# Seven products instead of eight for seven of the twelve column blocks of a SwiGLU

## The chip, the cores and the metric

The kernel runs on one core of one Trainium2 chip. The metric is the device time of one execution in microseconds, a median over runs. The core's engines work from queues of their own: PE multiplies matrices, DVE, ACT and POOL do elementwise work, SP issues most transfers.

## What is computed

Three layers follow one another on 1152 tokens of 512 values: a retention layer, a mixture of eight experts, and a SwiGLU. The change lies in the last one:

```
rms = np.sqrt(np.mean(x * x, axis=-1, keepdims=True) + 1e-06)
xn = x / rms * rms_g
g = xn @ w_gate                      # 1152x512 by 512x1536
silu = g * (1.0 / (1.0 + np.exp(-g)))
val = xn @ w_val                     # 1152x512 by 512x1536
return (silu * val @ w_out)          # 1152x1536 by 1536x512
```

The three weight matrices of this layer are float64 in memory; the result is float32.

## The kernel before

**Stages.** Attention and routing take the first 60 us or so, the experts run to about 214 us, the SwiGLU from there to the end. Only the last stage changes its work.

**Numbers in two parts.** Each float32 operand is split into a rounded high part (`xh`, `uh`, `sh`; ACT writes it) and the rest (`xl`, `ul`, `sl`; DVE subtracts it), and a product is three matmuls: high by high, high by low, low by high.

**Items.** The 1536 columns are twelve blocks `f` of 128, the tokens three groups `g` of 384. An item (g, f) is `gate_val` (L1120 to L1122: 24 matmuls of 384 columns, into one PSUM bank for gate and one for value, each held twice), `gate_act` (L1130 silu on ACT, L1132 the product on DVE, L1134 and L1136 the two parts) and `out_mm` two items later (L1154 to L1156: nine matmuls of 512 columns into three PSUM tiles). There are 36 items in three phases: f 0 and 1, f 2 to 5, f 6 to 11. At a phase's end `out_ev` moves the three tiles of a group into `parts` (ACT in phase 0, DVE afterwards), and in the last phase POOL scatters them to the output.

**Conversion.** For each f three units (gate, value, output weights) are fetched as 64-bit words (`st`, four buffers) and turned into float32 by `conv_u`: ACT takes the upper word's magnitude (L233), DVE masks the sign (L238) and joins the words (L249, L257), then ACT and DVE make `uh` and `ul` (L265, L268). The generator is cut into three steps a unit; `between` puts them among the four pieces of `gate_act`, so many an item as `G_OPS` says by phase. All of this order is written by hand: each engine executes what the program lists for it in that order.

## Time and profile before

| | us |
|---|---|
| median of 3 runs (450.11 to 454.2) | 450.31 |
| the profiled execution's own time | 449.34 |
| its span, first to last instruction | 447.6 |
| PE busy | 432.2 |

The trace shows one execution. A matmul's record overlaps the next one's; what a matmul costs in a row of them is the distance from its start to the next one's. The same holds for DVE, by a little. Where a row names a line, it is a line of the kernel before.

### The profile page before, as it was taken

The page shows a single profiled execution, that of the slowest core. Times are in us where ns is not written, and L with a number is a line of the kernel's source. Part 1 is how long each engine was busy: PE and PEld are TensorE (multiplying, and loading weights), DVE is VectorE, ACT ScalarE, POOL GpSimd, SP SyncE. Part 2 cuts the span into 40 slices and gives each one's busy share as a digit, 9 for nine tenths or more (in the row PEclk, how much of TensorE's full clock was granted, in tenths as well). Part 3 has the DMA queues.
Part 4 walks back from the last instruction along what each step waited for, and adds up shares of the span by engine and source line. Part 5 has one row for each costly group of instructions (what it writes and reads, how often), then busy time and mean ns, then how long its engine had stood idle before and what let it go on. Part 6 is the DMA issues. An engine that isn't in the chain of part 4 may idle for free.

```text
span 447.6 us, 7844 instructions
## 1 busy us (share of the span) xinstructions
PE 432.2 (97%) x2976; PEld 410.5 (92%) x2976; DVE 285.5 (64%) x677; ACT 211.0 (47%) x453; POOL 56.1 (13%) x45
## 2 busy tenths in 40 slices
PE   6999989899999999999999999999999999999994
PEld 5888879899999999999999999999999999999993
DVE  3899857668888878786498888784763113113212
ACT  3443335778787877764466665350531111111110
POOL 8005210122441101012000000000000002001102
PEclk9999999899999999999999999999999999999999
DMA  8989829976999897673045564351300001000101
GB/s 284 306 280 379 314 82 346 327 230 143 367 184 348 245 308 256 244 256 116 1 140 175 156 187 143 112 173 45 94 1 0 0 2 70 1 1 21 51 1 70
DMA packets 40446, 72.28 MB, mean 162 GB/s; under 512 B 3894, under 2 KB 16566, under 8 KB 40404
## 3 DMA queue, kind: packets, MB, share of 16 engines
q1 hardware_dynamic: 38580, 67.00, 47.3%
q0 software_dynamic: 1824, 4.75, 2.9%
q8 instruction: 24, 0.39, 0.4%
q14 instruction: 18, 0.15, 0.1%
HBM read 65.21 MB, written 6.52 MB: 160 GB/s over the span
## 4 chain that ended last, share of the span: by engine, by line
PE 81%; DMA 2%; POOL 0%; DVE 0%; issue 0%; POOLq 0%; ACT 0%; DVEq 0%
PE gv L1120 11%; PE gv L1121 11%; PE gv L1122 11%; PE acc L914 11%; PE hp L623 9%; PE o L1154 5%; PE o L1156 5%; PE o L1155 5%; PE acc L915 4%; PE hp L863 3%; DMA xr<-tab 2%; PE hp L865 1%; PE tp L828 1%; PE sp L980 1%; POOL out_dram L1169 0%; PE sp L960 0%
## 5 line engine op out<-in xcount | busy, mean ns | idle before, releaser
L1120 PE MATMUL gv<-xh,uh 128*128 128x384 f32 x280 | 94.8, 339 | 0.0
L1122 PE MATMUL gv<-xh,ul 128*128 128x384 f32 x280 | 94.6, 338 | 0.0
L1121 PE MATMUL gv<-xl,uh 128*128 128x384 f32 x280 | 94.6, 338 | 0.0
L914 PE MATMUL acc<-h,w2h 128*128 128x384 f32 (+6 forms) x256 | 73.2, 360 | 0.0
L915 PE MATMUL acc<-h,w2l 128*128 128x192 f32 (+6 forms) x256 | 62.1, 243 | 0.0
L1132 DVE TENSOR_TENSOR sg<-sg,gv 128x384 f32<-128x384 f32 x35 | 19.3, 551 | 63.8 <-PE gv L1122 59.6
L1120 PEld LDWEIGHTS gv<-xh,uh 128*128 128x128 f32 x280 | 52.6, 188 | 1.4
L1121 PEld LDWEIGHTS gv<-xl,uh 128*128 128x128 f32 x280 | 52.6, 188 | 1.4
L1134 ACT ACTIVATE sh<-sg 128x384 fp32r<-128x384 f32 x36 | 18.9, 526 | 73.2 <-DVE sg L1132 73.1
L1122 PEld LDWEIGHTS gv<-xh,ul 128*128 128x128 f32 x280 | 52.6, 188 | 0.0
L623 PE MATMUL hp<-xt,w1t 128*128 128x192 f32 (+6 forms) x336 | 51.2, 306 | 0.6 <-DVE fl L644 0.6
L915 PEld LDWEIGHTS acc<-h,w2l 128*128 128x128 f32 x256 | 49.8, 195 | 0.0
L914 PEld LDWEIGHTS acc<-h,w2h 128*128 128x128 f32 x256 | 49.0, 191 | 0.0
L623 PEld LDWEIGHTS hp<-xt,w1t 128*128 128x128 f32 x336 | 47.5, 190 | 1.0 <-ACT h L889 0.8
L1154 PE MATMUL o<-uh,sh 128*128 128x512 f32 x108 | 42.8, 396 | 0.0
L1156 PE MATMUL o<-uh,sl 128*128 128x512 f32 x108 | 42.7, 395 | 0.0
L1155 PE MATMUL o<-ul,sh 128*128 128x512 f32 x108 | 42.5, 393 | 0.0
L1130 ACT ACTIVATE sg<-gv 128x384 f32<-128x384 f32 x35 | 17.0, 487 | 49.4 <-PE gv L1122 49.4
L787 DVE TENSOR_TENSOR w2l<-w2t,w2h 128x1024 fp32r<-128x1024 f32 x32 | 38.9, 1214 | 0.1
L778 ACT ACTIVATE w2h<-w2t 128x512 fp32r<-128x512 f32 x64 | 36.5, 620 | 3.4 <-DVEq L735 3.4
L1169 POOL DMA_INDIRECT out_dram<-part,ids_sb x9 | 8.9, 984 | 215.1 <-DVE part L1167 214.2
L265 ACT ACTIVATE uh<-mag 128x512 fp32r<-128x512 f32 x36 | 22.6, 627 | 14.7 <-DVE mag L257 10.0
(172 smaller groups left out, 727.5 us busy)
## 6 DMA issues: line engine op xcount, KB each, us to landing
w1t<-in_moe_w_dram SPq DMA_DIRECT2D x16, 1024.0 KB, 10.0
w2t<-in_moe_w_dram SPq DMA_DIRECT2D x32, 512.0 KB, 6.4
...
```

The source lines that it names most:

```text
L265: nc.scalar.activation(out=uh[:, s, :], in_=mag, func=ACTF.Copy)
L623: nc.tensor.matmul(hp[:, a, 0:w], w1_t[e, j // 2][:, kk, f * FT:(f + 1) * FT], xt[:, kk, :], start=(kk == 0), stop=(kk == KD - 1))
L778: nc.scalar.activation(out=w2_s[e, j][0][:, a, :], in_=t[:, a, :], func=ACTF.Copy)
L787: nc.vector.tensor_tensor(out=lo, in0=t, in1=hi.bitcast(F32), op=ALU.subtract)
L914: nc.tensor.matmul(ac[d // 2][:, d % 2, 0:2 * w], hi[:, a, d * P:(d + 1) * P], h[:, a].rearrange("p s t -> p (s t)"), start=first, stop=Fa ...
L915: nc.tensor.matmul(ac[d // 2][:, d % 2, 0:w], lo[:, a, d * P:(d + 1) * P], h[:, a, 0, :], start=False, stop=last, skip_group_check=True)
L1120: nc.tensor.matmul(ps[:, 0:GT], w_h, x_h, start=(kk == 0), stop=False)
L1121: nc.tensor.matmul(ps[:, 0:GT], w_h, x_l, start=False, stop=False)
L1122: nc.tensor.matmul(ps[:, 0:GT], w_l, x_h, start=False, stop=(kk == KD - 1))
L1154: nc.tensor.matmul(o, a, uh[:, 2, :], start=(f == fs[0]), stop=False)
L1155: nc.tensor.matmul(o, a, ul[:, 2, :], start=False, stop=False)
L1156: nc.tensor.matmul(o, b, uh[:, 2, :], start=False, stop=(f == fs[-1]))
```

## The change

**What stays plain.** Blocks f 0 to 4 are computed as before, in two phases (f 0 and 1; f 2 to 4), 15 items. `G_OPS` is now 6 conversion steps an item in the first and 7 in the second, and no bound holds conversion back: all twelve blocks are converted while these items run. For f 5 to 11 the float32 words are not split but written to memory (`raw_d`) by SP and read again when they are needed.

**Blocks of products.** For f 5 to 11 the gate and value columns are one 2 by 2 matrix of blocks (gate or value, first or second half of the 512 inputs), and the tokens are taken in two groups (`GROUPS`): twice 256, then twice 320. Of each group and f, called a slot (14 in all), the four result blocks come from seven block products with sums and differences of blocks on both sides. `prod` is one of them, six matmuls of 256 or 320 columns. POOL makes the sums: `x_split` for the tokens (six instructions a half, two halves for each of four tables; ACT and DVE split the results) and `w_sums` for the weights (four instructions a slot). `w_hi`, `w_lo`, `o_hi`, `o_lo` split the weights anew in each slot, and small additions on PSUM (rows `r<-q,m` and `m<-q,m`) join the products. The output matmuls of slot k - 1 stand in two halves within slot k; in the last slot they run from the last tile down, and one of them is kept for the end.

**Small things.** The constants that only attention reads lie in a pool that is closed after it. In the first two slots an extra matmul of 320 columns is issued ahead of the products.

**The order on PE.** Of the plain form, a piece of one item; the names are the tiles written and read.

```order
L1156 MATMUL o<-uh,sl 128x512
L1120 MATMUL gv_5409<-xh,uh 128x384
L1121 MATMUL gv_5409<-xl,uh 128x384
L1122 MATMUL gv_5409<-xh,ul 128x384
L1120 MATMUL gv_5409<-xh,uh 128x384
```

A slot's middle in the change: a second product into q, output tiles of the slot before, a third product into q.

```order
L1283 MATMUL q<-xh_5145,tl 128x256
L1305 MATMUL o<-oh,sh 128x512
L1306 MATMUL o<-ol,sh 128x512
L1307 MATMUL o<-oh,sl 128x512
L1305 MATMUL o<-oh,sh 128x512
L1306 MATMUL o<-ol,sh 128x512
L1307 MATMUL o<-oh,sl 128x512
L1281 MATMUL q<-xh_4927,th 128x256
```

The runs of 384 columns have become runs of 256 (later 320), with the output matmuls between them.

**The order on ACT, sixth item.** Before, conversion, the three copies of a group, the next silu:

```order
L233 ACTIVATE mag<-st 128x512
L265 ACTIVATE uh<-mag 128x512
L1165 ACTIVATE part_4810<-o 128x512
L1165 ACTIVATE part_4811<-o 128x512
L1165 ACTIVATE part_4812<-o 128x512
L1130 ACTIVATE sg<-gv_5025 128x384
```

In the change (L238 and L271 are the lines L233 and L265 of before):

```order
L238 ACTIVATE mag<-st 128x512
L1204 ACTIVATE xh_5145<-xd 128x4x128
L271 ACTIVATE uh<-mag 128x512
L1179 ACTIVATE part_4844<-o 128x512
L1179 ACTIVATE part_4845<-o 128x512
L1179 ACTIVATE part_4846<-o 128x512
L1144 ACTIVATE sg<-gv_5080 128x384
```

A copy of `xd`, which POOL writes, now stands ahead of the rounding, the copies and the silu.

**The order on DVE.** A piece of the last phase before:

```order
L1132 TENSOR_TENSOR sg<-sg,gv_6415 128x384
L1136 TENSOR_TENSOR sl<-sg,sh 128x384
L1132 TENSOR_TENSOR sg<-sg,gv_6457 128x384
L1136 TENSOR_TENSOR sl<-sg,sh 128x384
L1132 TENSOR_TENSOR sg<-sg,gv_6508 128x384
```

A slot of 256 columns in the change:

```order
L1331 TENSOR_TENSOR sg_6062<-sg_6062,q 128x256
L1342 TENSOR_TENSOR sl<-sg_6062,sh 128x256
L1342 TENSOR_TENSOR sl<-sg_6063,sh 128x256
L1451 TENSOR_TENSOR r<-q,m_6194 128x256
L1244 TENSOR_TENSOR tl<-raw,th 128x512
L1244 TENSOR_TENSOR tl<-raw,th 128x256
L1467 TENSOR_TENSOR m_6194<-q,m_6194 128x256
L1244 TENSOR_TENSOR tl<-ss,th 128x1024
L1481 TENSOR_TENSOR sg_6170<-sg_6170,m_6194 128x256
L1265 TENSOR_TENSOR ol<-raw,oh 128x512
```

Two instructions an item have become ten a slot.

```diff
-G_OPS = (6, 5, 5)
+G_OPS = (6, 7)
+GROUPS = ((0, 256), (512, 320))
...
-    A_U, B_U = 2, 6
+    A_U, SF = 2, 5
+    B_U = SF - A_U
...
-        return "A" if f < A_U or A_U + B_U <= f < 2 * A_U + B_U else "B"
+        return "A" if f < A_U else "B" if f < SF else "R"
...
-            nc.scalar.activation(out=uh[:, s, :], in_=mag, func=ACTF.Copy)
+            if plain:
+                nc.scalar.activation(out=w2u[f][0][:, s, :], in_=mag, func=ACTF.Copy)
 
         def lo():
+            if not plain:
+                return
+            uh, ul = w2u[f]
             nc.vector.tensor_tensor(out=ul[:, s, :], in0=mag, in1=uh[:, s, :].bitcast(F32), op=ALU.subtract)
 
+        if not plain:
+            nc.sync.dma_start(out=raw_d[f, s][:], in_=mag)
         tail[0] = (hi, lo)
+        tail_u[0] = (f, s)
...
-    phases = [list(range(0, A_U)), list(range(A_U, A_U + PH1)), list(range(A_U + PH1, NF2))]
-    order = [(ph, g, f) for ph in range(3) for g in range(NG) for f in phases[ph]]
+    phases = [list(range(0, A_U)), list(range(A_U, SF))]
+    order = [(ph, g, f) for ph in range(2) for g in range(NG) for f in phases[ph]]
...
+    def x_split(g, i, pool):
+        t0, n = GROUPS[g]
+        hn = n // 2
+        hi, lo = x_t[g, i] = [pool.tile([P, 4, n], F32R, tag=f"x{v}{g}{i}", name=f"x{v}{g}{i}") for v in "hl"]
+        for c in range(2):
+            xa = rxp.tile([P, 2, 2, NMX // 2], F32, tag="xa", name="xa")[:, :, :, 0:hn]
+            xd = rxp.tile([P, 4, NMX // 2], F32, tag="xd", name="xd")[:, :, 0:hn]
+            for k in range(2):
+                src = [t[:, 2 * k + i, t0:t0 + 2 * n].rearrange("p (h c) -> p h c", h=2)[:, :, c * hn:(c + 1) * hn].bitcast(F32) for t in (xh, xl)]
+                nc.gpsimd.tensor_tensor(out=xa[:, k], in0=src[0], in1=src[1], op=ALU.add)
+            nc.gpsimd.tensor_tensor(out=xd[:, 0], in0=xa[:, 0, 1], in1=xa[:, 0, 0], op=ALU.subtract)
+            nc.gpsimd.tensor_tensor(out=xd[:, 2], in0=xa[:, 1, 1], in1=xa[:, 0, 1], op=ALU.subtract)
+            nc.gpsimd.tensor_tensor(out=xd[:, 1], in0=xa[:, 1, 1], in1=xd[:, 0], op=ALU.subtract)
+            nc.gpsimd.tensor_tensor(out=xd[:, 3], in0=xa[:, 1, 0], in1=xd[:, 1], op=ALU.subtract)
+            yield
+            hi_v, lo_v = (t[:, :, c * hn:(c + 1) * hn] for t in (hi, lo))
+            nc.scalar.activation(out=hi_v, in_=xd, func=ACTF.Copy)
+            yield
+            nc.vector.tensor_tensor(out=lo_v, in0=xd, in1=hi_v.bitcast(F32), op=ALU.subtract)
...
+    def load_raw(k, js):
...
+                    conv_tail()
+                t = rawp.tile([P, 512], F32, tag="raw", name="raw")
+                nc.sync.dma_start(out=t, in_=raw_d[f, j][:])
...
+    def w_sums(k):
+        if k >= len(slots):
+            return
+        gt, vt = raw_t[k, 0], raw_t[k, 1]
+        a11, a12, a21, a22 = gt[:, 0:256], gt[:, 256:512], vt[:, 0:256], vt[:, 256:512]
+        ss = ssp.tile([P, 4, 256], F32, tag="ss", name="ss")
+        ss_t[k] = ss
+        nc.gpsimd.tensor_tensor(out=ss[:, 0], in0=a21, in1=a22, op=ALU.add)
+        nc.gpsimd.tensor_tensor(out=ss[:, 2], in0=a11, in1=a21, op=ALU.subtract)
+        nc.gpsimd.tensor_tensor(out=ss[:, 1], in0=ss[:, 0], in1=a11, op=ALU.subtract)
+        nc.gpsimd.tensor_tensor(out=ss[:, 3], in0=a12, in1=ss[:, 1], op=ALU.subtract)
+
...
+    def prod(k, ps, w, b, first=False):
+        g = slots[k][0]
+        n = GROUPS[g][1]
+        th, tl = tw_t[k]
+        for i, (bh, bl) in enumerate(x_block(g, b)):
+            a, c = th[:, w, i * P:(i + 1) * P], tl[:, w, i * P:(i + 1) * P]
+            nc.tensor.matmul(ps[:, 0:n], a, bh, start=(first and i == 0), stop=False, skip_group_check=True)
+            nc.tensor.matmul(ps[:, 0:n], a, bl, start=False, stop=False, skip_group_check=True)
+            nc.tensor.matmul(ps[:, 0:n], c, bh, start=False, stop=(i == 1), skip_group_check=True)
...
+    def xs_all():
+        yield from x_split(0, 0, xq)
+        yield from x_split(0, 1, xq)
+        yield from x_split(1, 0, xq1[0])
...
-        between(gate_act(*order[i - 1]), G_OPS[it[0]], min(ready, NF2))
+        between(gate_act(*order[i - 1]), G_OPS[it[0]], NF2)
+        for _ in range(1 + (i in (3, 5))):
+            next(xs_gen, None)
...
+        if i == len(order) - 3:
+            w_sums(0)
+            load_raw(1, (0, 1))
+        if i >= len(order) - 3:
+            j = i - len(order) + 3
+            if j < 2:
+                w_hi(0, j)
+                w_lo(0, j)
     out_ev(*order[-1 - LAG])
     between(gate_act(*order[-1]), 0, NF2)
-    for t in range(3):
-        for it in order[-LAG:]:
-            out_mm(*it, (t,))
-            out_ev(*it, (t,))
+    w_hi(0, 2)
+    w_lo(0, 2)
+    w_sums(1)
+    load_raw(0, (2,))
+    for it in order[-LAG:]:
+        out_mm(*it)
+        out_ev(*it)
...
+    last_k = len(slots) - 1
+    for k, (g, f) in enumerate(slots):
+        n = GROUPS[g][1]
+        p, r = (psQ.tile([P, 512], F32, tag=t, name=t) for t in "pr")
+        sg = [gq.tile([P, NMX], F32, tag=f"sg{h}", name=f"sg{h}") for h in range(2)]
+        sm_t[k] = (sg, gq2.tile([P, 2 * NMX], F32R, tag="sh", name="sh"), gq2.tile([P, 2 * NMX], F32R, tag="sl", name="sl"))
+        if k:
+            act_1(k - 1)
+        q = psQ.tile([P, 512], F32, tag="o4" if n == 256 and k % 2 else "q", name="q")
+        if k < 2:
+
+            nc.tensor.matmul(q[:, 0:NMX], tw_t[k][0][:, 0, 0:P], xh[:, 0, 0:NMX], start=True, stop=True, skip_group_check=True)
+        prod(k, p, 0, "11", True)
+        prod(k, r, 3, "1", True)
+        nc.scalar.activation(out=q[:, 0:n], in_=p[:, 0:n], func=ACTF.Copy)
+        load_raw(k + 2, (0, 1))
+        if k:
+            s_hi(k - 1, 0)
+            s_lo(k - 1, 0)
+        m5 = gq.tile([P, NMX], F32, tag="m5", name="m5")
+        nc.scalar.activation(out=m5[:, 0:n], in_=r[:, 0:n], func=ACTF.Copy)
+        if k:
+            s_hi(k - 1, 1)
+            s_lo(k - 1, 1)
+        w_hi(k + 1, 0)
+        prod(k, p, 1, "21")
+        prod(k, q, 4, "2")
+        nc.scalar.activation(out=sg[0][:, 0:n], in_=p[:, 0:n], func=ACTF.Silu)
+        nc.vector.tensor_tensor(out=r[:, 0:n], in0=q[:, 0:n], in1=m5[:, 0:n], op=ALU.add)
+        w_lo(k + 1, 0)
+        w_hi(k + 1, 1)
+        w_lo(k + 1, 1)
+        ev_some(2)
+        w_hi(k + 1, 2)
+        if k in (2, 4):
+            next(xs_gen, None)
+        ts = list(o_tiles(k - 1)) if k else []
+        if k == last_k:
+            ts = ts[::-1]
+        if ts:
+            o_mm(k - 1, ts[:2])
+            ev_q.extend((k - 1, t) for t in ts[:2])
+        prod(k, q, 5, "3")
+        prod(k, r, 6, "22")
+        nc.vector.tensor_tensor(out=m5[:, 0:n], in0=q[:, 0:n], in1=m5[:, 0:n], op=ALU.add)
+        w_lo(k + 1, 2)
+        w_sums(k + 2)
+        o_hi(k)
+        load_raw(k + 1, (2,))
+        nc.scalar.activation(out=sg[1][:, 0:n], in_=r[:, 0:n], func=ACTF.Silu)
+        if k == last_k:
+            prod(k, q, 2, "4")
+        if ts:
+            o_mm(k - 1, ts[2:4] if k == last_k else ts[2:])
+            ev_q.extend((k - 1, t) for t in ts[2:])
+        if k < last_k:
+            prod(k, q, 2, "4")
+        c21_t[k] = q
+        nc.vector.tensor_tensor(out=sg[1][:, 0:n], in0=sg[1][:, 0:n], in1=m5[:, 0:n], op=ALU.mult)
+        o_lo(k)
+        ev_some(2)
+        if k in (0, 2, 4):
+            next(xs_gen, None)
+        if k in (1, 3):
+            bg_ops(3, NF2)
+    s_hi(last_k, 1)
+    s_lo(last_k, 1)
+    act_1(last_k)
+    s_hi(last_k, 0)
+    s_lo(last_k, 0)
+    for t in reversed(o_tiles(last_k)):
+        if t == 2:
+            o_mm(last_k - 1, [0])
+        o_mm(last_k, [t])
+        o_ev(last_k, [t])
+    es_l.close()
     es_g.close()
```

## Rows read from the trace of the kernel before

**Rows 1.** The page's busy times: engine, us busy, share of the span, instructions.

```profile
PE 432.2 (97%) x2976; PEld 410.5 (92%) x2976; DVE 285.5 (64%) x677; ACT 211.0 (47%) x453; POOL 56.1 (13%) x45
```

**Rows 2.** The page's chain that ended last: share of the span by engine.

```profile
PE 81%; DMA 2%; POOL 0%; DVE 0%; issue 0%; POOLq 0%; ACT 0%; DVEq 0%
```

**Rows 3.** Busy time by stretch: window, length, engines (x instructions), PEclk, DMA, GB/s.

```profile
30.00:35.00 5.00, 4.19 (x72) 3.69 (x70) 4.65 (x26) 1.63 (x5) 0.34 (x1) 1.00 1.05 394
225.20:250.50 25.30, 25.30 (x137) 24.08 (x136) 22.65 (x44) 16.72 (x31) 0.00 (x0) 1.00 0.52 167
...
320.00:434.00 114.00, 114.00 (x599) 106.68 (x598) 34.90 (x62) 23.17 (x45) 5.96 (x6) 1.00 0.04 15
```

**Rows 4.** Timeline of PE, last items: start us, us, engine, line, operation.

```profile
428.94 0.40 PE L1154 MATMUL o<-uh,sh 128*128 128x512 f32 x1
...
435.28 0.40 PE L1154 MATMUL o<-uh,sh 128*128 128x512 f32 x1
...
441.34 0.40 PE L1156 MATMUL o<-uh,sl 128*128 128x512 f32 x1
```

**Rows 5.** Timeline of PE, experts' second layer: pairs of two widths.

```profile
92.61 0.36 PE L914 MATMUL acc<-h,w2h 128*128 128x384 f32 x1
92.80 0.25 PE L915 MATMUL acc<-h,w2l 128*128 128x192 f32 x1
92.89 0.36 PE L914 MATMUL acc<-h,w2h 128*128 128x384 f32 x1
...
206.04 0.34 PE L914 MATMUL acc<-h,w2h 128*128 128x288 f32 x1
206.21 0.23 PE L915 MATMUL acc<-h,w2l 128*128 128x144 f32 x1
206.28 0.34 PE L914 MATMUL acc<-h,w2h 128*128 128x288 f32 x1
```

**Rows 6.** Groups by line and shape: xcount | busy us, mean ns | idle before.

```profile
L787 DVE TENSOR_TENSOR w2l<-w2t,w2h 128x1024 fp32r<-128x1024 f32 x32 | 38.9, 1214 | 0.1
L265 ACT ACTIVATE uh<-mag 128x512 fp32r<-128x512 f32 x36 | 22.6, 627 | 14.7 <-DVE mag L257 10.0 <-PE o L1156 4.5
```

**Rows 7.** Timeline of DVE, one unit's conversion and the items around it.

```profile
230.97 0.41 DVE L238 TENSOR_SCALAR sgn<-st 128x512 int32<-128x512 int32 x1
231.30 0.68 DVE L257 SCALAR_TENSOR_TENSOR mag<-st,mag 128x512 int32<-128x512 int32 x1
231.91 0.68 DVE L268 TENSOR_TENSOR ul<-mag,uh 128x512 fp32r<-128x512 f32 x1
232.51 0.55 DVE L1136 TENSOR_TENSOR sl<-sg,sh 128x384 fp32r<-128x384 f32 x1
232.98 0.68 DVE L249 SCALAR_TENSOR_TENSOR mag<-mag,sgn 128x512 int32<-128x512 int32 x1
...
247.61 0.68 DVE L249 SCALAR_TENSOR_TENSOR mag<-mag,sgn 128x512 int32<-128x512 int32 x1
249.59 0.56 DVE L1132 TENSOR_TENSOR sg<-sg,gv 128x384 f32<-128x384 f32 x1 [1.29 <-ACT sg L1130]
```

**Rows 8.** Timeline of DVE and POOL where both work; POOL alone; POOL's memset.

```profile
136.50 1.22 DVE L787 TENSOR_TENSOR w2l<-w2t,w2h 128x1024 fp32r<-128x1024 f32 x1
136.74 1.55 POOL L970 TENSOR_TENSOR s<-t,mhalf 90x2 f32<-90x2 f32 x1 [7.78 <-DVE t L969]
...
207.05 1.71 POOL L970 TENSOR_TENSOR s<-t,mhalf 74x2 f32<-74x2 f32 x1 [14.95 <-DVE t L969]
...
219.07 0.71 POOL L970 TENSOR_TENSOR s<-t,mhalf 72x2 f32<-72x2 f32 x1 [9.28 <-DVE t L969]
...
L519 POOL MEMSET xh<- 128x5376 uint32 x1 | 4.6, 4584 | 0.0
```

**Rows 9.** The end, DVE and POOL: the last tile's sum and its write.

```profile
441.78 0.69 DVE L1167 TENSOR_TENSOR part<-part,o 128x512 f32<-128x512 f32 x1 [0.72 <-PE o L1156]
442.74 0.97 POOL L1169 DMA_INDIRECT out_dram<-part,ids_sb  x1 [0.44 <-DVE part L1167]
```

More of the change, by code (lines that the diff above doesn't have):

```diff
@@ L181 @@
     ids_d = dram.tile([NT, 1], I32, name="ids_d")
+    raw_d = {(f, j): dram.tile([P, 512], F32, name=f"raw{f}_{j}") for f in range(SF, NF2) for j in range(3)}
     tab_v = dram_disjoint_views(tab[:], NTI)
@@ new lines, in o_ev, with ev_some @@
+    def o_ev(k, ts):
+        g, f = slots[k]
+        if f != NF2 - 1:
+            return
+        for t in ts:
+            i = GROUPS[g][0] // P + t
+            nc.vector.tensor_tensor(out=parts[i], in0=parts[i], in1=oq_t[g, t], op=ALU.add)
+            nc.gpsimd.indirect_dma_start(
+                out=out_v[i], out_offset=bass.IndirectOffsetOnAxis(ap=ids_sb[:, i:i + 1], axis=0),
+                in_=parts[i][:], in_offset=None)
+    c21_t, ev_q = {}, []
+    def ev_some(m):
+        for _ in range(min(m, len(ev_q))):
+            k, t = ev_q.pop(0)
+            o_ev(k, [t])
```

152 lines of the change are left out of this document (123 added, 29 removed).

## Prediction, made before the changed kernel ran

> **What bounds the kernel now.** I read the page's busy times first: PE 432.2 us of a span of 447.6 [rows 1]. Then the chain that ended last: PE holds 81% of it, DVE and ACT nothing [rows 2]. Then the busy time by stretch, where the stage of the change lies: PE is busy in all of it at a granted clock of 1.00, while DVE is busy 22.65 of 25.30 us at first and 34.90 of 114 late [rows 3]. So the stage is a row of matmuls without a gap, with a DVE that is nearly full while it converts weights and nearly idle afterwards. The change asks both for less of PE and for more of DVE and POOL in just these places, so the question is whether the row stays closed.
>
> **A matmul's price.** From one item's first output matmul to the next item's it is 435.28 - 428.94 = 6.34 us; the last 27 output matmuls start within 441.34 - 435.28 = 6.06 us, 26 steps of 0.233 [rows 4]. Nine of them are 2.10, which leaves 4.24 for 24 matmuls of 384 columns, 0.177 each. Between 384 and 512 columns that is 0.44 ns a column; on this line 256 columns cost 0.1205 us and 320 cost 0.1486. No row has these widths in a row of their own, so I bound them. In the experts a pair of 384 and 192 columns starts every 0.28 us and one of 288 and 144 every 0.24 [rows 5]. With 0.177 and 0.135 from the line for the wide ones, both narrow ones come to 0.105, the narrower at no less: that is a floor, and 256 lies above it. Bounds: 256 and 320 columns at the full 2.4 GHz (0.107 and 0.133), and what 32 columns more cost (0.135 and 0.163). I take the line, since the rows on both sides lie on it or above the floor.
>
> **PE.** Per block f, three plain items are 19.02 us. The two slots are 7 products of six matmuls at each width, 42 x (0.1205 + 0.1486) = 11.30, and the unchanged 27 output matmuls, 6.29: 17.59. Seven blocks save 7 x 1.43 = **10.0 us**. By the bounds it is 18.6 or 1.7. The two extra matmuls of 320 columns add **0.3**.
>
> **Slot 0** has no output matmuls of a slot before to put between its products. Product 3 may overwrite q only after DVE has added q to r. At the end of the kernel DVE starts 0.44 us after the start of the matmul it waits for [rows 4, 9]; a sum of 256 columns is some 0.35 (below), and the next matmul would otherwise have come after 0.12: some 0.7, with the way back **0.8 us**. In later slots six output matmuls, 1.4 us, cover it.
>
> **DVE while the plain items run.** On DVE I count by distances of starts: sign 0.33, joins 0.61 and 0.60, low part 0.60, an item's low part 0.47 [rows 7]; the item's product likewise. From the third plain item to the fifteenth the order lists 30 units (46.2 us), 9 low parts of plain weights (5.4), 14 items' two instructions (13.2), six sums into parts (3.7), six low parts of token sums (3.3) and the first slot's weights (2.1, with the 1024-wide low part at 1.21 less the overlap [rows 6]). That is 73.9 us within 13 x 6.34 = 82.4. So seven steps an item fit, with 8.5 to spare. What comes free at the last block's conversion later on (DVE had 34.90 of 114 us to do) is worth nothing, since PE did not wait there.
>
> **POOL is new.** Before, it did nothing of size here. Alone, an instruction on two columns took 0.71 us; beside a 1024-wide DVE instruction with two inputs, which had begun 0.24 us earlier, it took 1.55, to 0.57 after that one's end [rows 8]. Its memset wrote a word in 4584/5376 = 0.85 ns. So a 256-wide POOL instruction costs 0.93 us at least by these rows (0.71 + 256 words) and some 2.2 at most (1.55 and three streams). I take 1.15, two streams on the undisturbed row. The page GPSIMD Engine Reference of the Trainium skill (Performance versus the Vector engine) has 4497 ns for 2048 elements, which for 256 would make an estimate of 0.56. No row here shows such a size.
>
> At 1.15 one half of a token split is 2 x 1.15 + 4 x 0.93 = 6.0 us. At the sixth item ACT's copy of it stands ahead of the rounding, the group's copies and the silu. DVE was free there at 248.3 and took the item's product at 249.59 [rows 7]. Now: low part to 248.8, POOL to 254.8, copy, rounding and three copies at about 0.63 each (the rounding's 627 ns [rows 6]) to 258.0, silu and product to 259. PE wants that bank back two items later, about 256.9: 2.1 us lost, none if POOL is done in 3.9. DVE also waits, which uses most of its spare time. I take **1.5 us** for this stretch, between 0 and what the rival below gives.
>
> **The slots.** One lasts 42 x 0.1205 + 12 x 0.233 = 7.9 us, in the second group 42 x 0.1486 + 15 x 0.233 = 9.7. DVE's ten instructions, 1.0 ns a column and a little by rows 7, are 4.8 us; ACT's ten some 5, at 0.63 for 512 columns [rows 6]; POOL's four 4.6. All fit. Within a slot I follow the chain: the weights' sums of slot k + 2 wait until DVE has read those of k + 1 (one buffer), about 6.8 us in, and are done 3.5 us into the next slot. ACT comes to them at 3.7, and 4.6 still does no harm. Up to 1.45 us per POOL instruction, then, nothing is lost. Two more halves of token splits stand in this queue. I take **0.6 us** over all slots.
>
> **The end.** The three last tiles were written as PE gave them out, every 1.4 us. Now five tiles come at 0.70 us each from PE, with DVE at 0.69 and POOL at 0.97 [rows 9]: POOL's queue is late by the end, five writes from the first one that can start, some **0.9 us** more than before (0 to 2). The output product kept for the end covers the last ACT and DVE steps, which would otherwise stand open.
>
> **Costed at nothing.** The transfers: seven steps need 7/3 of 0.52 MB fetched and 0.26 written back, 1.84 MB per 6.34 us or 290 GB/s, where 394 were reached at a DMA share of 1.05; 167 are moved there now [rows 3]. If that cover goes, DVE's joins are late, four buffers deep. On SP each write waits for DVE's join and the fetch behind it wants the buffer that the same join frees, so nothing is added; in the slots a fetch that waits for DVE and POOL has the output weights behind it, which are wanted a slot later. The pools' new places and the divided constants move no instruction that PE waits for.
>
> **Sum:** -10.0 + 0.3 + 0.8 + 1.5 + 0.6 + 0.9 = -5.9 us. The profiled execution took 449.34 us, 0.97 below the median of the runs; against the median it is 450.31 - 5.9 = **444.4 us**.
>
> **Rivals.** *All covers hold* (POOL near 0.7 us an instruction): -10.0 + 0.3 + 0.8 + 0.5 gives about 442. For it: DVE's and ACT's sums leave room. Against it: no row of POOL at such a price on a wide operand. Chance 0.18.
>
> *The weights' sums set the slot.* At 1.7 us per POOL instruction, what it took in one row on two columns [rows 8], the chain is 1 us late in each of six slots of 256 columns: 6 us in place of 0.6, about 450; the second group has 1.8 us more room. Chance 0.14.
>
> *DVE becomes the bound of the plain items* (slower). POOL's work there is four halves of 6.0, two of 6.4 and two sets of weights' sums, some 46 us. Rows 8 show POOL waiting for DVE; whether DVE stands still for POOL, no row shows. If it does, it has 8.5 us to spare and some 3 of slack before the first slot wants its weights. From a quarter of POOL's time onward PE loses microsecond for microsecond: at one half, 23 us, the loss is 11.5 in place of 1.5, 454.4; at all of it, more than 470. Chance 0.15. The page SBUF — State Buffer of the Trainium skill (Who interferes with whom) says that a DVE instruction with two SBUF inputs and a GpSimd instruction that reads SBUF exclude one another for a whole instruction; the first half of that agrees with rows 8, the other half is this rival.
>
> *PE does not get the narrow price.* At the upper bound the saving is 1.7 in place of 10.0, about 452.7. The floor of 0.105 speaks against it. Chance 0.05.
>
> **How the numbers follow.** The forecast, 442.5 to 447.5, has 0.48. A measurement of this kernel tells about 1% from no change, 4.5 us: faster is below 445.8, slower above 454.8. Of the forecast about three quarters lie below 445.8, with the first rival 0.54; slower is most of DVE's rival, 0.14; the rest is 0.32. The range, 440.5 to 451, takes in the first rival's lower end and the weights' sums; DVE's rival and the upper matmul price stay out.
>
> **What would show it.** Right: matmuls of 256 columns starting every 0.12 us, of 320 every 0.15; PE without gaps over 0.3 us from the second slot on; a gap below 1 us in slot 0; POOL's last five writes back to back. Wrong: PE waiting for DVE's product in the plain items after the sixth; DVE's two-input instructions longer than their 0.68 us beside POOL; a first product into r that waits for the 1024-wide low part; and, above all, a matmul price of 256 columns at 0.135 or more.

## The result, and the profile after

The changed kernel took 457.69 us (median of 17 runs, 454.57 to 462.16); the kernel before, run beside it, 453.65 us (17 runs, 450.11 to 455.03). The ratio is 1.0096 [1.0067, 1.0124]: about 1% slower, where 1.3% faster was predicted. Part of the distance to the predicted 444.4 us is that the three runs shown first had a median 3.3 us below that of the larger set; the sign is wrong all the same.

The page's busy times and the chain that ended last, in the changed kernel:

```profile
PE 426.1 (93%) x3062; PEld 399.6 (88%) x3062; DVE 349.3 (77%) x762; ACT 244.7 (54%) x538; POOL 144.0 (32%) x149
...
PE 18%; POOL 6%; DVE 3%; DMA 3%; issue 1%; ACT 1%; POOLq 0%; SPq 0%; DVEq 0%
```

PE is busy 6.1 us less than in [rows 1], and still the span is 455.9 us in place of 447.6. The shares of the chain add up to 32% here, since the view follows it back to 303.59 us only (before: to 64.92), so PE's 18% is not to be set against the 81% of [rows 2]. But in the part that it covers POOL, DVE and transfers stand between the matmuls: the row is no longer closed.

I cut the last stage at four points of PE's timeline: its start is the third item's first gate matmul; then the plain **stretch** up to the extra matmul of slot 0; then the **slots** up to the last start of a matmul; then the **tail** to the end of the span. The stage's start lies at 225.20 us before and 227.84 after. Over all profiled executions of this study it lies between 223.3 and 232.5 us. In front of it the code does the same work in all kernels (but for the first fills of one experiment, said there), and so only what follows it is compared. From there to the end the kernel before took 222.4 us, the changed one 228.1 (93.06 stretch, 126.85 slots, 8.15 tail): 5.7 us more.

Busy time by stretch in the changed kernel (the columns of [rows 3]):

```profile
227.84:250.50 22.66, 22.66 (x122) 21.57 (x121) 22.59 (x35) 13.62 (x26) 11.36 (x14) 1.00 0.44 140
250.50:282.20 31.70, 28.53 (x149) 26.01 (x149) 26.00 (x46) 15.22 (x29) 12.76 (x18) 1.00 0.69 229
282.20:320.90 38.70, 34.53 (x172) 29.83 (x171) 36.22 (x63) 15.83 (x29) 7.38 (x10) 1.00 0.80 268
320.90:377.70 56.80, 54.25 (x370) 49.00 (x368) 46.43 (x72) 30.91 (x70) 36.56 (x42) 1.00 0.31 94
377.70:447.75 70.05, 70.05 (x412) 64.81 (x411) 44.78 (x79) 31.61 (x69) 24.82 (x29) 1.00 0.24 77
```

In the first of these windows DVE is full, 22.59 of 22.66 us, where before it was busy 22.65 of 25.30 [rows 3]; in the third it is busy 36.22 of 38.70, and PE stands idle for 4.2 us. In the second PE stands idle for 3.2 us although DVE is busy for only 26.00 of 31.70: there DVE waits itself. POOL, which stood still here before, is busy 11.36 us in the first. In the slots of 256 columns (the row from 320.90) PE is busy 54.25 of 56.80, in those of 320 it has no gap.

What PE waited for in the stretch (us in total, times, longest):

```profile
PE o L1168 <- ACT part L1179: 3.2, 2, 1.6
PE o L1168 <- DVE part L1181: 2.4, 2, 1.8
PE o L1168 <- ACT sh L1148: 1.6, 2, 1.2
```

These are banks not yet emptied and high parts not yet written: ACT and DVE came late to what PE wanted. Part of it is the wait that the prediction worked out for the sixth item (ACT's and DVE's waits in the stretch, same columns):

```profile
ACT xh L1204 <- POOL xd L1201: 4.5, 1, 4.5
DVE ul L277 <- ACT uh L271: 3.2, 1, 3.2
```

ACT's copy waits 4.5 us for POOL, behind it DVE 3.2 us for ACT's rounding, and PE then 1.6 us, at 257.66, for the bank that ACT copies. Now DVE where POOL works beside it, in one item, and POOL in the same microseconds (timelines; start, length):

```profile
240.96 0.68 DVE L254 SCALAR_TENSOR_TENSOR mag<-mag,sgn 128x512 int32<-128x512 int32 x1
...
242.59 0.95 DVE L262 SCALAR_TENSOR_TENSOR mag<-st,mag 128x512 int32<-128x512 int32 x1
243.46 0.95 DVE L277 TENSOR_TENSOR ul<-mag,uh 128x512 fp32r<-128x512 f32 x1
244.33 1.09 DVE L1150 TENSOR_TENSOR sl<-sg,sh 128x384 fp32r<-128x384 f32 x1
245.34 1.23 DVE L254 SCALAR_TENSOR_TENSOR mag<-mag,sgn 128x512 int32<-128x512 int32 x1
...
246.83 0.68 DVE L262 SCALAR_TENSOR_TENSOR mag<-st,mag 128x512 int32<-128x512 int32 x1
```

```profile
242.34 0.64 POOL L1200 TENSOR_TENSOR xd<-xa,xd 128x128 f32<-128x128 f32 x1
243.06 0.79 POOL L1201 TENSOR_TENSOR xd<-xa,xd 128x128 f32<-128x128 f32 x1
243.93 2.09 POOL L1197 TENSOR_TENSOR xa<-xh,xl 128x256 f32<-128x256 f32 x2
```

The join of L254 (before: L249) takes 0.68 us at 240.96 and the join of L262 (before: L257) 0.68 at 246.83, as in [rows 7]. Between them, while POOL runs sums, the same kinds of instructions take 0.95 (twice), 1.09 in place of 0.55, and 1.23. This is the question that [rows 8] left open: DVE's instructions do get longer beside POOL's.

The matmuls themselves. PE's timeline in a slot of 256 columns:

```profile
328.01 0.28 PE L1282 MATMUL r<-xl,th 128*128 128x256 f32 x1
328.13 0.28 PE L1283 MATMUL r<-xh,tl 128*128 128x256 f32 x1
```

and in one of 320:

```profile
387.65 0.31 PE L1282 MATMUL r<-xl,th 128*128 128x320 f32 x1
387.80 0.31 PE L1283 MATMUL r<-xh,tl 128*128 128x320 f32 x1
```

The starts are 0.12 and 0.15 us apart, the means over the products of all slots 0.120 and 0.146, against 0.1205 and 0.1486 worked out from [rows 4].

The end, POOL's writes (before: [rows 9]):

```profile
446.03 0.98 POOL L1316 DMA_INDIRECT out_dram<-part,ids_sb  x1 [19.11 <-DVE part L1315]
447.32 0.96 POOL L1316 DMA_INDIRECT out_dram<-part,ids_sb  x1 [0.30 <-issue]
...
451.10 0.96 POOL L1316 DMA_INDIRECT out_dram<-part,ids_sb  x1 [0.30 <-issue]
```

Five writes follow one another 1.26 us apart, each 0.96 and 0.30 of issue. The tail is 8.15 us long against 6.26 before.

### The profile page after: what moved, and what is told of

Read it like the earlier page. It is cut to its first block, busy times and chain, and to the rows that moved or that the text cites. A ratio compares the mean times of both kernels' runs of the same rounds, so it can differ in the third digit from the quotient of the medians.

```text
span 455.9 us, 8507 instructions
## 1 busy us (share of the span) xinstructions
PE 426.1 (93%) x3062; PEld 399.6 (88%) x3062; DVE 349.3 (77%) x762; ACT 244.7 (54%) x538; POOL 144.0 (32%) x149
## 5 line engine op out<-in xcount | busy, mean ns | idle before, releaser
L1134 PE MATMUL gv<-xh,uh 128*128 128x384 f32 x112 | 37.8, 337 | 0.0
L1135 PE MATMUL gv<-xl,uh 128*128 128x384 f32 x112 | 37.6, 336 | 0.0
L1136 PE MATMUL gv<-xh,ul 128*128 128x384 f32 x112 | 37.6, 336 | 0.0
L238 ACT ACTIVATE mag<-st 128x512 f32<-128x512 f32 x36 | 23.7, 668 | 12.5 <-DMA st<-in_moe_w_out_dram 6.3
L254 DVE SCALAR_TENSOR_TENSOR mag<-mag,sgn 128x512 int32<-128x512 int32 x36 | 27.6, 767 | 0.2
L262 DVE SCALAR_TENSOR_TENSOR mag<-st,mag 128x512 int32<-128x512 int32 x36 | 26.6, 740 | 0.1
L1305 PE MATMUL o<-oh,sh 128*128 128x512 f32 x63 | 24.9, 396 | 1.4 <-ACT sh L1336 1.4
L1281 PE MATMUL q<-xh,th 128*128 128x256 f32 (+1 forms) x84 | 25.1, 299 | 0.6 <-DVE r L1451 0.6
L1307 PE MATMUL o<-oh,sl 128*128 128x512 f32 x63 | 24.9, 396 | 0.2 <-DVE sl L1342 0.2
L1168 PE MATMUL o<-uh,sh 128*128 128x512 f32 x45 | 18.3, 407 | 7.2 <-ACT part L1179 3.2
L1306 PE MATMUL o<-ol,sh 128*128 128x512 f32 x63 | 24.8, 394 | 0.0
```

Source lines behind the costliest of these rows:

```text
L1134: nc.tensor.matmul(ps[:, 0:GT], w_h, x_h, start=(kk == 0), stop=False)
L1135: nc.tensor.matmul(ps[:, 0:GT], w_h, x_l, start=False, stop=False)
L1136: nc.tensor.matmul(ps[:, 0:GT], w_l, x_h, start=False, stop=(kk == KD - 1))
L1281: nc.tensor.matmul(ps[:, 0:n], a, bh, start=(first and i == 0), stop=False, skip_group_check=True)
L1305: nc.tensor.matmul(o, a, oh, start=(f == SF), stop=False)
L1306: nc.tensor.matmul(o, a, ol, start=False, stop=False)
```

## The experiments

One table first; the texts below say what each kernel is. All numbers but the last column are from PE's timeline of one profiled execution, in us; the last is the ratio of the times to the kernel before, run on the same chip beside it. How much a stretch varies from one execution of a kernel to the next was not measured, so a difference of 1 to 3 us between two rows rests on one trace of each.

| kernel | stretch | slots | tail | stage | ratio to before |
|---|---|---|---|---|---|
| before | | | 6.26 | 222.4 | 1 |
| changed | 93.06 | 126.85 | 8.15 | 228.1 | 1.0096 [1.0067, 1.0124] |
| e1_no_split | 83.93 | 123.39 | 8.14 | 215.5 | 0.9862 [0.9825, 0.9899] |
| e2_no_store | 90.49 | 126.52 | 8.15 | 225.2 | 1.0125 [1.0049, 1.0201] |
| e3_neither | 83.66 | 123.23 | 8.17 | 215.1 | 0.9815 [0.9734, 0.9896] |
| e4_single | 91.93 | 126.48 | 8.18 | 226.6 | 1.0146 [1.0069, 1.0222] |
| e5_unread | 94.33 | 126.46 | 8.14 | 228.9 | 1.0113 [1.0069, 1.0158] |
| e6_memset | 87.28 | 123.26 | 8.18 | 218.7 | 0.9927 [0.9884, 0.9970] |
| v4 | 90.05 | 131.96 | 8.17 | 230.2 | 1.0137 [1.0104, 1.0170] |
| v2 | 83.65 | 137.16 | 8.11 | 228.9 | 1.0145 [1.0116, 1.0173] |
| v9 | 86.83 | 141.30 | 8.16 | 236.3 | 1.0348 [1.0294, 1.0402] |
| v10 | 89.74 | 138.12 | 8.14 | 236.0 | 1.0320 [1.0262, 1.0377] |
| v12 | 83.65 | 126.73 | 8.20 | 218.6 | 0.9937 [0.9899, 0.9976] |
| v13 | 89.80 | 124.19 | 8.14 | 222.1 | 1.0013 [0.9974, 1.0052] |

### Which part of the change costs the time

Three parts could: POOL's token sums, the new traffic of raw words, and the order in which ACT stands behind POOL. Where the expectations of these four runs give 95.7 us for the stretch of the changed kernel and 84.5 for one without stalls, they count from 225.2 us, the start in the kernel before; from the changed kernel's own start these are 93.06 and 83.7.

**e1_no_split** leaves the token sums out: ACT and DVE split slices of the tokens in their place.

```diff
-                nc.gpsimd.tensor_tensor(out=xa[:, k], in0=src[0], in1=src[1], op=ALU.add)
-            nc.gpsimd.tensor_tensor(out=xd[:, 0], in0=xa[:, 0, 1], in1=xa[:, 0, 0], op=ALU.subtract)
...
+            xd = xh[:, :, t0 + c * hn:t0 + (c + 1) * hn].bitcast(F32)
```

> Leaves out POOL's token sums, in the plain items and in the slots: ACT and DVE split slices of the tokens' high part instead, with the same shapes (48 POOL instructions less). In the changed kernel the plain stretch, from the third item's first matmul at 225.2 us to slot 0's at 320.9, takes 95.7 us; its matmuls alone are 84.5. Theory P (POOL costs the stretch its time: DVE stands still while POOL works, and ACT waits behind POOL at the sixth item): the stretch falls to 88 or less, slots 3 and 5 lose their 1.3 and 2.5 us, the whole is 10 to 12 us faster than the changed kernel. Theory D (the float words that are written out take the transfers' time, so the 64-bit words come late): the stretch stays at 93 or more, the whole gains 4 to 6 us, all in the slots.

With the token sums left out, the time falls by as much as was predicted for the whole change (ratio 0.9862, predicted 0.987): the stretch is 9.1 us shorter than in the changed kernel, the slots 3.5. Its windows (stretch, slots of 256 columns):

```profile
232.54:316.47 83.93, 83.93 (x439) 77.99 (x438) 76.78 (x142) 44.99 (x83) 5.54 (x5) 1.00 0.74 247
316.47:371.30 54.83, 54.23 (x380) 50.60 (x379) 42.76 (x73) 31.50 (x72) 25.46 (x31) 1.00 0.31 98
```

PE is busy in all of the stretch. DVE is busy 76.78 us there; in the changed kernel the windows of the stretch sum to 84.81.

**e2_no_store** leaves the 21 writes of raw words out; the slots read other words of the same size.

```diff
-            nc.sync.dma_start(out=raw_d[f, s][:], in_=mag)
...
-                nc.sync.dma_start(out=t, in_=raw_d[f, j][:])
+                nc.sync.dma_start(out=t, in_=w1[f % E, j * P:(j + 1) * P, 0:512])
```

> Leaves out the 21 writes of the float words; the slots read words of another float32 input of the same size instead, so that reads stay as many. Theory P: the stretch stays at 92 to 96 us, the whole moves by less than 3 us. Theory D: fetches land in 4 us or less instead of up to 8.4, the stretch falls to 88 or less, the whole is 7 us or more faster.

**e3_neither** has both edits.

> Leaves out both, POOL's token sums and the writes. If P and D are two separate costs of the same full DVE, the stretch comes to 84.5 to 86 us, more than either alone gives, and the whole is 13 to 15 us faster than the changed kernel, near 443. If one of them is the whole cause, this equals that one alone.

The writes are worth 2.6 us of the stretch where POOL makes sums (93.06 against 90.49), and 0.3 where it doesn't (83.93 against 83.66). With the writes gone DVE's waits for fetched words fall from 3.5 to 0.3 us in the stretch. The ratio of e2, 1.0125 [1.0049, 1.0201], does not tell it from the changed kernel, so the 2.6 us stand on the traces alone; either way the writes are not the main cause.

**e4_single** takes one step of a token split an item; the changed kernel took two in the items with i = 3 and 5.

```diff
-        for _ in range(1 + (i in (3, 5))):
+        for _ in range(1):
             next(xs_gen, None)
```

> Takes away only the double steps of the token sums at the fourth and sixth items, so that ACT's copy never stands right behind POOL's work; POOL's work is the same, 13 steps in 13 items. If ACT behind POOL (3.2 us of DVE idle at 254 to 257, PE's wait of 1.6 us at 257.7) is what PE loses, the stretch gets 3 us shorter. If DVE is full anyway because it stands still for POOL, under 1.5 us.

1.1 us of the stretch, less than the 1.5 that was set as the line. DVE's wait for ACT's rounding is gone, but DVE is busy 87.35 us in place of 84.81, so most of it is taken up again: where the steps stand matters little.

### Waiting for POOL's results, or standing still beside POOL

So the token sums cost some 9 us in the stretch and 3.5 in the slots. In the trace both kinds of loss are there: ACT waited 4.5 us at one place for POOL's table, and DVE's instructions grew. Two kernels part them.

**e5_unread**: POOL makes all sums, and nobody reads them.

```diff
             hi_v, lo_v = (t[:, :, c * hn:(c + 1) * hn] for t in (hi, lo))
+            xd = xh[:, :, t0 + c * hn:t0 + (c + 1) * hn].bitcast(F32)
```

> POOL makes the token sums as in the changed kernel, but ACT and DVE read slices of the tokens in their place, so that nobody waits for POOL's token sums (the sums' use is left out). Counted from the stage's start (third item's first gate matmul, 227.84 us in the changed kernel) to slot 0's extra matmul, the changed kernel took 93.06 us, without token sums 83.93. Theory C (DVE's two-input instructions stand still while POOL reads SBUF): the stretch stays at 89 to 92 us, and DVE's subtraction on 512 columns (low parts) still lasts 0.75 us or more on average; total 451 to 456 us. Theory W (ACT and DVE stand in their queues for POOL's results): the stretch falls to 84 to 85.5 us, total 446 to 449 us. In the slots the split of the last table no longer makes ACT or DVE wait, but POOL still comes late to the weights' sums by its 6 us: slots 126 us as in the changed kernel (126.85).

The stretch is 94.33 us, no shorter, and longer than the 89 to 92 that theory C gave. POOL, for which nobody waits now, runs its sums close together (windows):

```profile
228.77:250.50 21.73, 21.72 (x117) 20.48 (x115) 21.66 (x27) 11.52 (x22) 21.10 (x26) 1.00 0.35 108
250.50:323.10 72.60, 66.93 (x322) 59.45 (x323) 67.22 (x117) 33.55 (x63) 14.07 (x16) 0.95 0.76 254
```

POOL is busy 21.10 of 21.73 us and DVE 21.66, yet DVE gets through 27 entries of this view there, where the changed kernel has 35 in 22.66. By group, in the stretch:

```profile
L254 DVE SCALAR_TENSOR_TENSOR mag<-mag,sgn 128x512 int32<-128x512 int32 x30 | 24.1, 805 | 0.1
...
L1150 DVE TENSOR_TENSOR sl<-sg,sh 128x384 fp32r<-128x384 f32 x14 | 9.6, 683 | 0.6 <-ACT sh L1148 0.6
L277 DVE TENSOR_TENSOR ul<-mag,uh 128x512 fp32r<-128x512 f32 x9 | 8.4, 937 | 0.0
```

DVE's subtraction L277 takes 937 ns, the low part L1150 683. Part of the 94.33 us is PE's clock. PE after its longest wait, and a window of it:

```profile
262.71 0.79 PE L1168 MATMUL o<-uh,sh 128*128 128x512 f32 x1 [2.85 <-ACT part L1179]
...
265.75 0.52 PE L1135 MATMUL gv<-xl,uh 128*128 128x384 f32 x1
266.07 0.52 PE L1136 MATMUL gv<-xh,ul 128*128 128x384 f32 x1
```

```profile
263.00:268.00 5.00, 5.00 (x15) 4.42 (x15) 4.87 (x10) 4.17 (x9) 0.00 (x0) 0.50 0.46 154
```

The granted clock was 0.50 here, and sixteen matmuls (six of 512 columns, ten of 384) took 5.89 us, from 262.71 to 268.60, where 6 x 0.233 + 10 x 0.177 = 3.17 would be the price at 1.00. Less these 2.7 us the stretch would be 91.6, an estimate: within theory C, and 1.5 us shorter than in the changed kernel. So the waits for POOL's results are worth something, but in this kernel POOL's closer work on DVE takes it back.

**e6_memset**: POOL fills the same tiles, each three times over, and reads nothing; all wait for it as in the changed kernel.

```diff
-                nc.gpsimd.tensor_tensor(out=xa[:, k], in0=src[0], in1=src[1], op=ALU.add)
-            nc.gpsimd.tensor_tensor(out=xd[:, 0], in0=xa[:, 0, 1], in1=xa[:, 0, 0], op=ALU.subtract)
...
+            for k in (0, 1) * 3:
+                nc.gpsimd.memset(xa[:, k], 0.5)
+            for k in (0, 2, 1, 3) * 3:
+                nc.gpsimd.memset(xd[:, k], 0.5)
```

> POOL's token sums are replaced by fills of the same tiles, each three times over (some 4.3 us a half, worked out from a fill of 512 words at 0.52 us, in place of some 4.9), so POOL is occupied about as long and everyone waits for it as in the changed kernel, but it reads nothing (the token sums are left out). Theory C (DVE stands still where POOL reads): the stretch falls to 84 to 86 us from 93.06, low parts on 512 columns are back at about 0.70 us, and total is 447 to 450 us. Theory W (waiting for POOL's results): the stretch stays at 89 to 92 us, total 452 to 457. Slots in both: weights' sums late behind the fills as before, 125 to 127 us.

The stretch falls to 87.28 us, and the slots to 123.26 (125 to 127 were expected), as without any token sums. The stretch is 1.3 us above the upper end that was expected and 3.4 above that of e1. DVE is busy there for 77.65 us, hardly more than e1's 76.78, but its 3.2 us of waiting for ACT's rounding, which stands behind POOL's table, is still there, and PE waits in the last two items, 1.16 and 0.46 us for ACT's high part. So of the 9.1 us some 5.8 go with the reading, and 3.4 are left where POOL only writes and is waited for. The fills kept POOL less long than the sums (22.7 us in the stretch against 31.5), and the first of them ran ahead of the stage, from 219.91 us, since they read no tokens; so they match POOL's time only in part. The same groups of DVE, first in the changed kernel:

```profile
L254 DVE SCALAR_TENSOR_TENSOR mag<-mag,sgn 128x512 int32<-128x512 int32 x30 | 23.5, 784 | 0.1
L262 DVE SCALAR_TENSOR_TENSOR mag<-st,mag 128x512 int32<-128x512 int32 x30 | 22.5, 751 | 0.0
...
L1150 DVE TENSOR_TENSOR sl<-sg,sh 128x384 fp32r<-128x384 f32 x14 | 9.3, 664 | 0.6 <-ACT sh L1148 0.6
...
L277 DVE TENSOR_TENSOR ul<-mag,uh 128x512 fp32r<-128x512 f32 x9 | 7.1, 785 | 3.2 <-ACT uh L271 3.2
```

then with fills:

```profile
L254 DVE SCALAR_TENSOR_TENSOR mag<-mag,sgn 128x512 int32<-128x512 int32 x30 | 21.1, 704 | 0.1
L262 DVE SCALAR_TENSOR_TENSOR mag<-st,mag 128x512 int32<-128x512 int32 x30 | 21.1, 703 | 0.0
...
L1150 DVE TENSOR_TENSOR sl<-sg,sh 128x384 fp32r<-128x384 f32 x14 | 8.3, 591 | 0.6 <-ACT sh L1148 0.6
...
L277 DVE TENSOR_TENSOR ul<-mag,uh 128x512 fp32r<-128x512 f32 x9 | 6.2, 687 | 3.2 <-ACT uh L271 3.2
```

784, 751, 664 and 785 ns become 704, 703, 591 and 687; in e1, without token sums, they are 703, 687, 590 and 685. What lengthens DVE is that POOL reads, not that it is busy or waited for. The page SBUF — State Buffer of the Trainium skill (Who interferes with whom) states just this: a DVE instruction with two SBUF inputs contends with a GpSimd instruction that reads SBUF and not with one that only writes it. These two runs agree. The reverse shows in the same trace of e6. POOL's weights' sums, and DVE's entry in the same microseconds:

```profile
311.07 0.73 POOL L1224 TENSOR_TENSOR ss<-raw 128x256 f32<-128x256 f32 x1 [21.99 <-DVE tl L1241]
```

```profile
310.91 1.88 DVE L1181 TENSOR_TENSOR part<-part,o 128x512 f32<-128x512 f32 x3
```

Beside a DVE instruction with one input in PSUM, a sum of 256 columns takes POOL 0.73 us. In the changed kernel the four lines of such sums average 784 to 955 ns.

### Other places for the sums

**v4** keeps four halves of token sums in the stretch, one step an item, and puts the other four, in pieces of two POOL instructions, behind the weights' sums of slots 0 to 5.

```diff
-        yield from x_split(1, 0, xq1[0])
...
         w_sums(k + 2)
+        xf(k, True)
```

> Token sums of the second group leave the plain stretch: four halves stay there, one step an item; the other four are cut into pieces of two POOL instructions, two pieces behind the weights' sums of each of slots 0 to 5. Nothing is left out. By the loss per half (9.4 us of stalls for six halves and the rest) the stretch should fall from 93.06 to about 89 us if POOL's time beside DVE is the cause (both theories), and the slots from 126.85 to 123.5 to 125 us, since the weights' sums no longer stand behind 6 us of token sums at once. Total about 457.7 - 4 - 2.5 = 451 us, ratio to before 0.995. If the pieces push the weights' sums late in every slot, the slots stay at 127 or more and the total at 454 or above.

The stretch went down 3.0 us, the slots up 5.1, not down: PE waits 3.1 us there, in three places, for DVE's m (`m<-q,m`), and 1.6 for ACT's copy of q. **v2** is v4 with six steps an item in the second phase and two more units in the slots.

```diff
-G_OPS = (6, 7)
+G_OPS = (6, 6)
...
-        if k in (1, 3):
-            bg_ops(3, NF2)
+        bg_ops({0: 3, 1: 3, 2: 3, 3: 3}.get(k, 0), NF2)
```

> As the variant with the second group's token sums in the slots, and besides six conversion steps an item in the second phase in place of seven: four units (12 steps) of the last blocks are converted in slots 0 to 3 in place of two. DVE then has 4.6 us less in the nine items of the second phase (9 steps of about 0.51 us), and the transfers are spread. If the stretch is bound by DVE (its own work plus what POOL takes of it), its stalls fall by about as much: stretch 85 to 87 us, slots 124 to 125.5, total 446 to 449 us. If what DVE waits for in the stretch are POOL's results, six steps change nothing: stretch 89 us, total as in the variant with seven steps.

Its stretch has no stall at all, shorter than expected, and its slots take 137.16, where 124 to 125.5 were expected. Windows of the stretch and of slots 0 to 6:

```profile
224.78:308.43 83.65, 83.65 (x439) 78.15 (x438) 77.94 (x130) 41.16 (x78) 24.80 (x31) 1.00 0.72 235
308.43:374.50 66.07, 58.60 (x369) 50.98 (x368) 56.10 (x82) 33.81 (x75) 42.95 (x49) 0.95 0.30 98
```

The stage is 228.1, 230.2 and 228.9 us in the changed kernel, v4 and v2. What is taken out of the stretch comes back in the slots. In v2 DVE is busy 56.10 of 66.07 us there, beside 42.95 us of POOL; whether its amount of work or the order of it holds PE up, these two runs do not part.

### DVE makes the token sums itself

If POOL's reading takes about as much of DVE as the sums are worth, DVE can as well make them, in wide instructions. **v9** does so, with six steps an item and the fourth table in the slots:

```diff
-                nc.gpsimd.tensor_tensor(out=xa[:, k], in0=src[0], in1=src[1], op=ALU.add)
+                nc.vector.tensor_tensor(out=xa[:, k], in0=src[0], in1=src[1], op=ALU.add)
...
+        next(xs_gen, None)
+        bg_ops({0: 3, 1: 3, 2: 3, 3: 3}.get(k, 0), NF2)
```

> DVE makes the token sums itself, in instructions of 512 and 256 columns (group 0) and 640 and 320 (group 1), in place of POOL; POOL keeps the weights' sums. Three tables in the plain stretch, the fourth in slots; the second phase takes six conversion steps an item, and four units are converted in slots 0 to 3. Nothing is left out. DVE pays 2 x 0.68 + 4 x 0.42 = 3.05 us per table of group 0 and about 3.6 per table of group 1. Without token sums DVE was busy 76.8 of 83.9 us in the stretch and 42.8 of 54.8 in slots 0 to 6. Theory C (in the changed kernel POOL's reading takes as much of DVE as the sums themselves would cost, and DVE's total is the limit): stretch 76.8 + 9.7 - 4.6 = 82 us busy, so 84 to 86 long (changed kernel: 93.06); slots 0 to 6 busy 42.8 + 3.6 + 3.1 = 49.5 of 54.8, so 124 to 126 us for all slots (126.85); total 447 to 451 us, ratio to before 0.985 to 0.995. If instead moving the work to DVE costs more than POOL took of it, the stretch stays above 90 us and the total above 454.

**v10** keeps seven steps and puts two tables into the slots.

```diff
-        yield from x_split(1, 0, xq1[0])
...
+    def xs_late():
+        yield from x_split(1, 0, xq1[0])
+        yield from x_split(1, 1, xq1[1])
```

> DVE makes the token sums itself as in the variant above, seven conversion steps an item as in the changed kernel (two units in slots 1 and 3), and both tables of group 1 are made in slots 0 to 5, one step a slot. Nothing is left out. Theory C: stretch 76.8 + 6.1 - 1.6 = 81.3 us of DVE, 84 to 85.5 long; slots 0 to 6 busy 42.8 + 7.2 + 0.9 = 50.9 of 54.8, 124 to 127 us for all slots; total 447 to 451 us. If a long run of DVE instructions in a slot delays what PE waits for there (its product, its low parts), the slots are 128 or more and the total 452 or more.

Both missed by far in the slots, 141.30 and 138.12 us, and v10 in the stretch as well, 89.74 where 84 to 85.5 were expected. In v9's trace of DVE, at the end of a slot:

```profile
324.79 2.65 DVE L1199 TENSOR_TENSOR xa<-xh,xl 128x640 f32<-128x640 f32 x2
327.36 1.21 DVE L254 SCALAR_TENSOR_TENSOR mag<-mag,sgn 128x512 int32<-128x512 int32 x1
328.50 0.94 DVE L243 TENSOR_SCALAR sgn<-st 128x512 int32<-128x512 int32 x1
329.36 0.68 DVE L262 SCALAR_TENSOR_TENSOR mag<-st,mag 128x512 int32<-128x512 int32 x1
329.96 0.41 DVE L1334 TENSOR_TENSOR sg<-sg,q 128x256 f32<-128x256 f32 x1
```

and what PE did meanwhile:

```profile
330.87 0.50 PE L1308 MATMUL o<-oh,sh 128*128 128x512 f32 x1 [4.03 <-ACT sh L1339]
```

DVE's product (`sg<-sg,q`), for which ACT's high part and PE's output matmuls wait, comes at 329.96, behind 5.2 us of token sums and conversion that stand ahead of it; PE loses 4.03 us. In slots 0 to 6 (317.54:376.00) DVE is busy 45.34 of 58.46 us: it is not full, it works on the wrong thing first. The granted clock is 0.88 in this window, so some of the loss is matmuls after such waits at a lower clock. **v12** has v9's amount of work. In the slots the table is cut into single instructions and the units into single steps, spread over slots 0 to 6, and in the stretch ACT's copy comes an item after DVE's sums.

```diff
         w_lo(k + 1, 0)
+        bg_ops(NB.get(k, 0) > 0, NF2)
         w_hi(k + 1, 1)
         w_lo(k + 1, 1)
+        bg_ops(NB.get(k, 0) > 1, NF2)
...
+        next(xs_gen, None)
         w_hi(k + 1, 2)
```

> DVE makes the token sums as in the variant with six steps an item, three tables in the stretch, but ACT's copy of a table comes one item after DVE's sums, so that ACT's silu no longer stands behind them; in the slots the fourth table is cut into ten pieces of one instruction and the four units into single steps, spread over slots 0 to 6 behind what PE waits for, in place of up to 5 us of DVE work at the end of a slot. Nothing is left out. If the losses of the two variants before (slots 9 to 15 us longer) came from where the work stood in DVE's queue and not from its amount, the stretch is 84.5 to 86 us and the slots 124 to 128, total 446 to 451 us, ratio to before 0.985 to 0.995. If DVE's amount is the limit there (42.8 us without sums, plus 4.9 for the table, plus 6 for four units, of 54.8), slots are 130 or more and the total 453 or more.

**v13** is v12 with seven steps an item and six single steps in the slots.

> As the variant above, but seven steps an item in the second phase and two units in slots 0 to 3 (six single steps). Nothing is left out. Stretch: DVE busy 76.8 + 9.7 = 86.5 us, so 87.5 to 90 long; slots 123.5 to 126; total 448 to 453 us. Shorter than the variant above if DVE's amount limits the slots, longer by 2 to 4 us if it does not.

v12 has a closed stretch, 83.65 us, and slots of 126.73; v13 89.80 and 124.19. v12 is the one version here that leaves nothing out and beats both kernels, the one before with a ratio of 0.9937 [0.9899, 0.9976]. Its windows of the stretch and of slots 0 to 6:

```profile
225.92:309.57 83.65, 83.65 (x439) 78.14 (x438) 79.73 (x147) 42.17 (x77) 7.22 (x7) 1.00 0.70 234
309.57:365.20 55.63, 53.67 (x362) 47.51 (x361) 48.54 (x87) 32.86 (x73) 24.70 (x25) 1.00 0.38 117
```

DVE is busy 79.73 of 83.65 us and PE does not wait once. v13 adds four units, some 1.5 us each by [rows 7] without their low parts: 79.73 + 6.1 is more than 83.65. DVE is busy 84.90 us in v13's stretch, and PE waits 2.8.

## Why the prediction was wrong

| term of the sum | predicted | measured | from |
|---|---|---|---|
| PE, extra matmuls, slot 0 | -10.0 + 0.3 + 0.8 = -8.9 | -8.8 | e1's stage 215.5 - 222.4, less 1.9 of tail |
| the plain stretch | +1.5 | +9.1 | 93.06 - 83.93 |
| the slots | +0.6 | +3.5 | 126.85 - 123.39 |
| the end | +0.9 | +1.9 | 8.15 - 6.26 |
| sum | -5.9 | +5.7 | |

**What held.** The price of narrow matmuls, read off a line between two widths, was right to 2% (0.120 and 0.146 us); slots came out at 7.8 and 9.6 us where 7.9 and 9.7 were worked out; slot 0 lost 0.60 us to DVE's r. The rival of the full price is refuted, and so is that of the weights' sums as what sets the slot: without token sums every slot of the first group, from the second on, takes 7.8 to 8.0.

**The step that failed** is "I take **1.5 us** for this stretch". It measured 9.1. The term held one wait, at the sixth item, and put the lengthening of DVE's instructions beside POOL at nothing, leaving it to a rival. That rival, "DVE becomes the bound of the plain items", came true, at a chance of 0.15, and with the mechanism it named. Two of its numbers can be corrected now. DVE was busy 84.81 us in the stretch and 76.78 without token sums: 8.0 us were lost beside 31.50 - 5.54 = 26.0 us more of POOL than in e1, three tenths, and not the half for which 454.4 was worked out. The share is not fixed: in e5 it is 12.1 us beside 29.6, four tenths. And POOL's work in the stretch came to 31.5 us, not 46. A loss of 8.0 us lies within the 8.5 us that I called spare, and still PE lost 9.1. In e1 DVE stood idle 83.93 - 76.78 = 7.2 us, 3.8 of it waiting for transfers and 2.4 for ACT's silu; in the changed kernel it stood idle 93.06 - 84.81 = 8.3, no less: 3.5 for transfers, 0.4 for the silu, and 3.2 that are new, for the rounding behind POOL's table. A sum of durations set against a window does not say that the rest can be filled: the queue is in order, and waits stand where the order puts them. With less conversion in the stretch and no token sums of POOL beside it, v12 has a closed row with 3.9 us of DVE idle. That the rival's 454.4, 4.1 us above the kernel before, is near the measured 4.0 is luck: it had 11.5 us in the stretch and none of what the slots and the end cost beyond their terms.

The wait that the term did hold came as worked out, 1.6 us of PE at the sixth item where 1.5 were taken, though POOL took some 4.6 us a half, not 6.0. It is the smaller part: with such waits gone (e4; e5, less what its lower clock cost) the stretch is 1.1 and some 1.5 us shorter, with the waits kept and the reading gone (e6) 5.8. POOL's instruction, taken at 1.15 us from an undisturbed row and memset's rate, is 0.73 alone. The estimate of 0.56 worked out from the page GPSIMD Engine Reference of the Trainium skill (Performance versus the Vector engine) was too low by about a quarter of that. So the unknown I spent most words on, POOL's price, did little harm, and the one I gave a chance to, what POOL takes of DVE, decided.

**The slots.** The prediction saw that "two more halves of token splits stand in this queue" and gave all slots 0.6 us. Slots 3 and 5 lost 1.3 and 2.5 us. POOL was 6.0 us at each half (331.25 to 337.26 and 348.40 to 354.40 on its timeline), and the weights' sums behind it came late by so much. As sums that nobody reads (e5) the halves cost the same 126.5, as fills of 4.0 us each (321.55 to 325.50 in e6) nothing. This fits weights' sums that come late behind the halves, where some 4 us of delay pass and 6 do not. A rival stands beside it: the fills do not read, and DVE, beside halves that do, is busy 91.20 us in all slots in place of e1's 87.31; these runs do not part the two, and what part of the 6 us POOL itself stood still for DVE was not measured.

**The end.** Writes were taken at 0.97 us, the record of one [rows 9]; five in a row stand 1.26 apart. Four distances of 0.29 more are 1.2 us, which is about what the term missed (1.9 for 0.9).

**Transfers**, costed at nothing, were nearly that: 0.3 us (e3 against e1), and 2.6 only with DVE late, by one trace each.

What stays open: why POOL's reading takes three tenths of its time from DVE in one order and four tenths in another was not taken apart instruction by instruction; how the 9.1 us divide between reading and waiting is known only as far as e4 to e6 go, which change both; nor was it tried whether POOL's weights' sums, which v12 still has, should move as well.
